# A recurrent layer's boot taken by halves, and a second layer that lags one, two, then three steps

## The chip, the cores and the metric

The kernel runs on one core of a Trainium2 chip. The metric is the device time of one execution, in microseconds (us). It is taken as the median over several executions; a profiled execution beside them gives the trace. In the trace a core has the engines TensorE (PE, with its weight loads as PEld), VectorE (DVE), ScalarE (ACT), GpSimd (POOL) and SyncE (SP), which issues most transfers.

## What is computed

The input is `r, k, v, w` of shape (4, 8, 768, 48) and `u` of shape (8, 48): four sequences, eight heads, 768 tokens, 48 numbers a head. Each head has a state of 48 x 48 that decays by `w` per token. Its result goes through two matrix products with a slight non-linearity between.

```python
for t in range(S):
    cur = einsum('bhd,bhe->bhde', u[None] * kt, vt)
    y[:, :, t] = einsum('bhd,bhde->bhe', rt, state + cur)
    state = wt[:, :, :, None] * state + einsum('bhd,bhe->bhde', kt, vt)
x = y.transpose(0, 2, 1, 3).reshape(3072, 384)
h = x @ w_in            # w_in: 384 x 2048
out = (h - tanh(h)) @ w_out   # w_out: 2048 x 384
```

## The kernel before

The 3072 tokens are cut into eight blocks of 384 (`NB`), two per sequence. Within a block the recurrence works on chunks of 64 tokens (`L`), six per block, and on four pairs of heads (`NPAIR`), a pair filling the partitions. Pairs come in two halves of two (`HALVES` is first pairs 2 and 3, called h1, then 0 and 1, called h2).

For a block the recurrence has these pieces. `behind` (L395) scans w backwards for the decay to the end of each chunk, `take_whole` (L421) picks each chunk's whole decay, `before` (L388) scans forwards from its reciprocal. `times_behind` and `times_before` (L413, L407) multiply them into k and r, and `times_u` (L425) multiplies k by u on ScalarE, in place, after `times_behind` has read it. `gram` (L448) forms the scores of a chunk with itself on TensorE: `own` for a token with itself, `earlier` for earlier tokens; a masked copy on VectorE (L470) puts them into the tile `scores`. `turn` (L481) transposes the decayed keys on TensorE and copies them out on ScalarE into `ks`. `update_1` (L521) multiplies keys and values into each chunk's contribution to the state, for all pairs; `update_2` (L541) walks over the chunks on VectorE, an add and a multiply each. `from_states` and `from_scores` (L591, L610) add up a block's result in PSUM, with a drain and a semaphore (`fence`) between the parts; `result_out` (L645) copies it into the tiles `xT`, and `fill_holes` (L657) moves the rest of the heads, from the tile `late`, by six small transfers.

A block's dense part is a loop of 16 steps f (`NF`), each for 128 of the 2048 middle columns. `first` (L764) does the first layer: three products (six records in the trace) into the single PSUM buffer `hp`, which ScalarE empties into `h`. `slight` (L776) makes g of h: the square s (VectorE, L796), qa (ScalarE, L799), and two products on VectorE (L773). The second layer, in block 0 `Second.add` (L841), multiplies g by `w_out`. In blocks 1 to 7 a scheme with fewer products takes its place (`Fewer`, L877).

The order on every engine but POOL is that of the program text (`manual_schedule`). In the loop (L1121) each step issues, in this order: what was put ahead of h (qa of the step before), `first`, this step's VectorE work, ScalarE's conversion of weights, the next block's pieces of recurrence that `plan` (L945) puts at this step, transfers, and then the second layers that are due. A second layer of block 0 is due three steps after its first layer (L1166, `LAG` 2 plus one).

The weights come as 64-bit patterns and are converted on the chip: `convert` (L249) has three ScalarE pieces and one combining VectorE operation per f. Five buffers hold raw weights. Three of the sixteen conversions lie in the boot, one in step 0 and the rest in steps 1 to 12, each three steps ahead of its use.

`boot` (L1010) prepares block 0, with nothing dense to hide behind. It loads w, k and r by halves, and v; it works the two halves one after the other until the scores, and takes `update_1`, `update_2` and `from_states` for all four pairs at once. `passed` (L288) puts 97 tiny products ahead of the first turn, and `busy` (L281) puts filler products in some places. Before it, memsets and masks are prepared: VectorE sets `scores`, `states` and `ones`, POOL draws all masks, also those which only the general path reads. That path (L1242) is a branch at the end that recomputes everything if a bound was broken; it isn't taken here.

## Time and profile before

| what | us |
|---|---|
| runs | 556.38, 558.57, 558.08 |
| their median | 558.08 |
| the profiled execution | 556.46 |
| its span, first to last instruction | 554.7 |
| first layer of step 0 starts | 29.47 |
| first second layer starts | 40.60 |
| last second layer's records start | 549.21 |

The mean granted clock of TensorE is 0.997. A line of the timeline gives start and duration in us, the engine, the line of the kernel, the operation, the tile written and the tiles read, shapes, and the number of records; in brackets the engine's idle time before and who ended it. A line of the table by windows gives a stretch, its length, the busy time of PE, PEld, DVE, ACT and POOL with their records, the granted clock, the share of the transfer engines and GB/s. Ends of products are modelled, so the distance of two starts is the better measure of what one costs.

### The profile page before, as it was taken

How to read it: one execution, taken by the hardware profiler on the slowest of the kernel's cores; microseconds unless marked ns; L12 is line 12 of the kernel's file. 1: busy time of each engine (PE TensorE's matmuls, PEld its weight loads, DVE VectorE, ACT ScalarE, POOL GpSimd, SP SyncE). 2: the span in 40 equal slices, each digit the busy share in tenths (PEclk: the TensorE clock that was granted, in tenths of full speed). 3: DMA queues.
4: the chain of work that ended last, by engine and by line, in shares of the span. 5: the costliest groups of instructions: out<-in, count | busy, mean ns of one | idle time of the engine just before them, and what ended most of it. 6: DMA issues, size and time to landing. Idle time of an engine off the chain costs nothing.

```text
span 554.7 us, 14151 instructions
## 1 busy us (share of the span) xinstructions
PE 537.9 (97%) x5726; PEld 404.7 (73%) x5726; DVE 463.3 (84%) x947; ACT 402.2 (73%) x811; POOL 12.0 (2%) x40
## 2 busy tenths in 40 slices
PE   4899999999999999999999999999999999999996
PEld 4646566578787787777778787777877777787774
DVE  8789999989989989878997989969897897557563
ACT  3889896697766886688866886688865986666561
POOL 6100000000000000000000000000000000000000
PEclk9999999999999999999999999999999999999999
DMA  8598473244302432236311531136122320100101
GB/s 304 207 320 301 165 215 107 72 122 115 116 13 85 100 118 74 62 94 134 109 54 44 144 116 62 52 89 157 58 88 67 80 65 4 54 1 0 44 2 46
DMA packets 53030, 56.31 MB, mean 102 GB/s; under 512 B 21472, under 2 KB 50912, under 8 KB 52960
## 3 DMA queue, kind: packets, MB, share of 16 engines
q1 hardware_dynamic: 52576, 55.18, 33.6%
q8 instruction: 46, 0.75, 0.5%
q14 instruction: 24, 0.20, 0.1%
q10 hardware_dynamic: 288, 0.10, 0.1%
q0 software_dynamic: 96, 0.07, 0.1%
HBM read 44.73 MB, written 4.72 MB: 89 GB/s over the span
## 4 chain that ended last, share of the span: by engine, by line
PE 94%; ACT 2%; DVE 2%; issue 1%; DMA 1%; SPq 0%; DVEq 0%; ACTq 0%
PE hp L767 44%; PE acc L891 26%; PE att L891 6%; PE acc L844 6%; PE att L463 2%; PE att L603 2%; PE att L620 2%; PE acc L869 2%; PE att L537 2%; DMA r<-in_rT 1%; ACT up L260 1%; PE att L487 1%; DVE scores L470 0%; PE att L285 0%; DVE pre L392 0%
## 5 line engine op out<-in xcount | busy, mean ns | idle before, releaser
L767 PE MATMUL hp<-xT,w_sb 128*128 128x384 f32 x768 | 270.1, 488 | 1.3 <-ACT h L770 1.1
L767 PEld LDWEIGHTS hp<-xT,w_sb 128*128 128x128 f32 x768 | 137.3, 190 | 75.9 <-ACT h L770 3.3
L770 ACT ACTIVATE h<-hp 128x384 f32<-128x384 f32 x128 | 62.7, 490 | 104.8 <-PE hp L767 104.7
L891 PE MATMUL acc<-forms,g 128*128 128x128 f32 x954 | 133.7, 276 | 0.5
L891 PEld LDWEIGHTS acc<-forms,g 128*128 128x128 f32 x954 | 121.6, 192 | 10.3 <-issue 1.3
L773 DVE SCALAR_TENSOR_TENSOR h<-h,s 128x384 f32<-128x384 f32 x128 | 70.7, 552 | 53.9 <-ACT s L788 53.8
L814 DVE TENSOR_TENSOR g<-g 128x256 f32<-128x256 f32 x265 | 103.3, 419 | 7.8 <-PE acc L891 7.0
L789 ACT ACTIVATE qa<-s,shift 128x384 f32<-128x384 f32 x113 | 69.6, 616 | 3.7
L791 ACT ACTIVATE junk<-s,shift 128x384 bf16<-128x384 f32 x113 | 67.7, 600 | 0.0
L773 DVE SCALAR_TENSOR_TENSOR g<-qa,h 128x384 f32<-128x384 f32 x112 | 61.7, 551 | 1.8 <-ACT qa L799 0.2
L788 ACT ACTIVATE s<-h 128x384 f32<-128x384 f32 x113 | 59.1, 523 | 3.6
L891 PEld LDWEIGHTS acc<-w_sb,g 128*128 128x128 f32 x318 | 46.7, 191 | 9.7 <-ACT sums L859 0.3
L891 PE MATMUL acc<-w_sb,g 128*128 128x128 f32 x318 | 53.1, 276 | 0.1
L891 PE MATMUL att<-w_sb,g 128*128 128x128 f32 x212 | 35.5, 275 | 0.0
L891 PEld LDWEIGHTS att<-w_sb,g 128*128 128x128 f32 x212 | 31.1, 192 | 5.3
L926 DVE TENSOR_TENSOR sums<-sums 128x256 f32<-128x256 f32 x84 | 32.9, 408 | 1.6 <-ACT sums L903 1.3
L844 PE MATMUL acc<-w_sb,sums 128*128 128x384 f32 x96 | 33.9, 489 | 0.1
L260 ACT ACTIVATE up<-raw 128x768 f16<-128x768 f32 (+1 forms) x32 | 32.0, 1070 | 0.0
L392 DVE TENSOR_TENSOR_SCAN pre<-w,start 128x780 f32<-128x780 f32 x16 | 28.5, 1783 | 0.5
L403 DVE TENSOR_TENSOR_SCAN post<-w,seed 128x780 f32<-128x780 f32 x16 | 28.5, 1783 | 0.2 <-DMA w<-in_wT 0.2
L844 PEld LDWEIGHTS acc<-w_sb,sums 128*128 128x128 f32 x96 | 17.9, 190 | 12.0 <-issue 0.2
L791 ACT ACTIVATION_READ_ACCUMULATOR junk<-s,shift 128x1 f32 x113 | 21.1, 187 | 0.0
(93 smaller groups left out, 506.5 us busy)
## 6 DMA issues: line engine op xcount, KB each, us to landing
raw<-in_weights SPq DMA_DIRECT2D x16, 768.0 KB, 5.8
w<-in_wT SPq DMA_DIRECT2D x7, 780.0 KB, 4.6
k<-in_kT SPq DMA_DIRECT2D x7, 768.0 KB, 4.5
r<-in_rT SPq DMA_DIRECT2D x7, 768.0 KB, 4.5
v_sb<-in_v SPq DMA_DIRECT2D x8, 576.0 KB, 3.9
k<-in_tokens SPq DMA_DIRECT2D x7, 576.0 KB, 3.9
r<-in_tokens SPq DMA_DIRECT2D x7, 576.0 KB, 4.9
out_y<-sums SPq DMA_DIRECT2D x18, 128.0 KB, 1.8
```

The source lines that it names most:

```text
L260: return lambda: nc.scalar.activation(out=to, in_=of, func=AF.Copy, scale=scale, bias=bias)
L392: return nc.vector.tensor_tensor_scan(out=self.tile("pre")[:, cols], data0=self.tile("w")[:, cols], data1=start[:, 0:n * NCH * LP], initia ...
L767: nc.tensor.matmul(hp, lhsT=w_in_sb[:, f, kc, :], rhs=xT[kc], start=(kc == KC - 1), stop=(kc == 0))
L770: return h, nc.scalar.activation(out=h, in_=hp, func=AF.Copy, scale=1.0 / UPSCALE)
L773: return lambda: nc.vector.scalar_tensor_tensor(out=out, in0=in0, scalar=scalar, in1=in1, op0=op0, op1=ALU.mult)
L788: nc.scalar.activation(out=s, in_=h, func=AF.Square)
L789: nc.scalar.activation(out=qa, in_=s, func=AF.Square, bias=shift[:, 4:5])
L791: nc.scalar.activation(out=junk[:, 0:NB], in_=s, func=AF.Relu, bias=shift[:, 5:6], accum_out=excess[:, at:at + 1])
L814: return lambda: nc.vector.tensor_tensor(out=G[:, to:to + 2], in0=two(G, g_at(q, a0), g_at(q, a1)), in1=two(G, g_at(q, b0), g_at(q, b1)), ...
L844: nc.tensor.matmul(acc, lhsT=g[:, j * P:(j + 1) * P], rhs=w_out_sb[:, f, :], start=(f == self.first), stop=(f == NF - 1))
L891: nc.tensor.matmul(to, lhsT=G[:, g_at(q, a), :], rhs=rhs, start=start, stop=stop, skip_group_check=True)
L926: ops.append(lambda op=op, at=at: nc.vector.tensor_tensor(out=at[0], in0=at[1], in1=at[2], op=OPS[op]))
```

## The change

- The boot loads w of h1 in two transfers, starts with one weight load instead of three, and begins three more behind ScalarE operations. `behind` runs for one pair at a time in h1.
- Each half has its own update (`update_half`), with a drain and a wait between its two passes over a pair of heads. The states of a half come from one scan per pair over 48 x 6 elements (`states_half`), for which ScalarE spreads the decays by column (`totals_by_column`). `from_states` reads these states, six elements apart. A half's result is finished before the other's.
- `own` goes ahead of `turn` in h1, whose copy (`turn_2`) comes later. `passed` is gone. All hole transfers go on SP.
- ScalarE sets `scores` and two small tiles by copies of zeros; the padding columns of `states` are set only in the general path, which also draws masks 1, 2, 4 and 8.
- Conversions in the loop begin one step earlier in number (f + 3 from f = 0), with two of the three ScalarE pieces in one step and the third at the start of the next, for f below 8. One conversion is carried from the boot into step 0.
- In steps 0 to 3 of block 0 square, qa and both products are issued in the step itself, behind the combining operation, and the second layer is due one step later; for steps 4 to 7 two, then three.

```diff
+SOON = 4
...
-    nc.gpsimd.memset(mask_all[0:L], 1.0)
...
+    draw(("diagonal", "above"), slice(0, 128))
...
-    nc.vector.memset(A, 0.0)
+    nc.scalar.copy(out=A.rearrange("s h p c t -> s (h p c t)").rearrange("s (n t) -> s n t", t=BANK),
+                   in_=start[:, 0:BANK].unsqueeze(1).to_broadcast([P, 2 * NPAIR * NCP * L // BANK, BANK]))
...
-        nc.vector.memset(st[:, :, :, D:], 0.0)
...
+        def update_half(self, ps, p0):
+            self.by_column = scratch(ps)[:, :, 0:D * NCH].rearrange("d p (e c) -> d p e c", c=NCH)
+            for x in range(UP):
+                if x:
+                    nc.tensor.drain().then_inc(fence, 1)
+                    fences.append(None)
+                    nc.tensor.wait_ge(fence, len(fences))
+                for c in range(0, NCH, 2):
+                    for h in range(2):
+                        for par in range(2):
+                            p = (x + par) % UP
+                            toks = slice(64 * par, 64 * par + 64)
+                            e0 = (p0 + p) * D2 + h * D
+                            nc.tensor.matmul(self.by_column[64 * h:64 * h + 64, p, :, (c + par + 1) % NCH],
+                                             lhsT=self.ks[toks, p0 + p, c // 2, 64 * h:64 * h + 64],
+                                             rhs=self.v[toks, c // 2, e0:e0 + D], start=True, stop=True)
+        def totals_by_column(self, p0):
+            of = self.whole(p0, UP).rearrange("d (p c) -> d p c", c=NCH)[:, :, 1:]
+            nc.scalar.copy(out=first_totals[:, p0:p0 + UP, :, 1:],
+                           in_=of.unsqueeze(2).to_broadcast([P, UP, D, NCH - 1]))
+        def states_half(self, p0):
+            for p in range(UP):
+                to, by, kv = (t.rearrange("d e c -> d (e c)") for t in
+                              (first_states[:, p0 + p], first_totals[:, p0 + p], self.by_column[:, p]))
+                nc.vector.tensor_tensor_scan(out=to, data0=kv, data1=by, initial=0.0, op0=ALU.add, op1=ALU.mult)
+            return lambda kv=self.by_column: nc.vector.tensor_tensor(
+                out=states[1][:, p0:p0 + UP, 0, 0:D], in0=first_states[:, p0:p0 + UP, :, NCH - 1],
+                in1=kv[:, :, :, 0], op=ALU.add)
...
+        blk.behind(h1 + 1, 1)
+        blk.behind(h1, 1)
         blk.take_whole(h1, UP)
+        blk.totals_by_column(h1)
         blk.before(h1, UP)
         blk.times_behind(h1, UP)
         blk.times_u(h1, UP)
-        blk.turn(ps, h1, ahead=97)
         own = blk.own(ps, h1)
+        blk.turn_1(ps, h1)
         blk.times_before(h1, UP)
         earlier = blk.earlier(ps, h1)
         blk.bound(h1)
         blk.bound(h2)
+        blk.turn_2(h1)
+        blk.update_half(ps, h1)
         blk.behind(h2, UP)
         blk.take_whole(h2, UP)
+        blk.totals_by_column(h2)
         own()
         blk.times_behind(h2, UP)
...
+        begin_behind(blk.times_u(h2, UP), more_weights(nc.sync))
         first_a, first_b = convert(*raws.pop(0))
+        run(first_a[:1])
+        blk.turn_1(ps, h2)
+        begin_behind(blk.turn_2(h2), more_weights(nc.sync))
         second_a, second_b = convert(*raws.pop(0))
         third_a, third_b = convert(*raws.pop(0))
...
+        earlier()
+        blk.results(ps, halved=True)
+        blk.result("from_scores", both[0])
+        blk.states_half(h1)()
+        blk.result("from_states", both[0], True)
+        run(first_a[1:2])
+        blk.before(h2, UP)
+        own = blk.own(ps, h2)
+        blk.update_half(ps, h2)
+        blk.times_before(h2, UP)
+        earlier = blk.earlier(ps, h2, ahead=3)
+        blk.result_out((3,), nc.scalar.copy)
+        blk.fill_holes([nc.sync])
+        later.load("w")
+        run(first_a[2:])
+        blk.result_out((2,), nc.scalar.copy)
         own()
...
+        onwards = blk.states_half(h2)
+        blk.results(ps, halved=True)
+        busy(blk.yp[0][:, 0], 4)
+        blk.result("from_states", both[1])
         earlier()
...
+        onwards()
+        run(second_a[:1])
+        begin_behind(second_a[1](), more_weights(nc.sync))
+        run(second_a[2:])
         run(first_b)
         blk.result("from_scores", both[1], True)
...
+        busy(scratch(ps)[:, 0], 2)
+        begin_behind(third_a[0](), more_weights(nc.sync))
+        later.load("k")
         blk.result_out((1,), nc.scalar.copy)
         blk.result_out((0,), nc.vector.tensor_copy)
...
+        return third_a[2:], third_b
...
-            if i == 0 and f in (1, 2, 3):
+            if i == 0 and f == 1:
                 busy(acc[0], 2)
...
+            if not i:
+                run(carried[0])
+                extra = carried[1]
+            if not i and f < SOON:
+                run(square + ahead_of_h)
+                ops, later_ops, ahead_of_h = extra + later_ops + behind, [], []
+            elif not i:
                 ops = rest + square + formed + extra + behind
...
             if f + READY in converted:
-                ops, extra = convert(*raws.pop(0))
-                for op in ops:
-                    op()
-            elif f:
-                extra = []
+                ops, carried = convert(*raws.pop(0)), []
+                some_now = 2 if f < 2 * SOON else 3
+                run(ops[0][:some_now])
+                carried = ops[0][some_now:], ops[1]
...
-                due.append((now + LAG + (not i), second.add if later else second.added, (f, g)))
+                due.append((now + (LAG if i else 1 if f < SOON else 2 if f < 2 * SOON else 3),
+                            second.add if later else second.added, (f, g)))
```

152 lines of the change are left out of this document (65 added, 87 removed).

## The prediction

> **What bounds the kernel now.** I read the page first (engines and slices), then the table by windows for the start, then the timeline of the first 60 us, and the chain of waits last.
>
> ```profile
> PE 537.9 (97%) x5726; PEld 404.7 (73%) x5726; DVE 463.3 (84%) x947; ACT 402.2 (73%) x811; POOL 12.0 (2%) x40
> ...
> PE   4899999999999999999999999999999999999996
> ```
>
> TensorE is busy for 97% of the span, and only the first slice (13.9 us each) and the last show anything else. The table by windows (stretch, length, then PE, PEld, DVE, ACT, POOL busy, granted clock, DMA share, GB/s) shows where:
>
> ```profile
> 0.00:5.00 5.00, 2.58 (x97) 2.47 (x97) 3.54 (x14) 1.49 (x2) 4.30 (x18) 1.00 0.55 178
> 5.00:10.00 5.00, 0.64 (x3) 0.64 (x4) 4.82 (x6) 0.66 (x2) 4.80 (x6) 1.00 1.03 341
> ...
> 35.00:40.00 5.00, 4.07 (x13) 2.16 (x14) 4.40 (x8) 5.00 (x8) 0.00 (x0) 1.00 0.98 358
> 40.00:50.00 10.00, 10.00 (x41) 6.37 (x40) 9.65 (x19) 9.99 (x16) 0.00 (x0) 1.00 0.92 319
> 50.00:60.00 10.00, 10.00 (x108) 6.19 (x107) 9.56 (x17) 9.28 (x15) 0.00 (x0) 1.00 0.65 209
> ```
>
> From 40 us on TensorE never stops, so the change can win or lose only in what lies before: the boot, and block 0's first steps. But in block 0 VectorE (9.6 of 10) and ScalarE (9.3 to 10 of 10) are nearly full as well. The timeline (start, duration, engine, line) gives the marks:
>
> ```profile
> 4.31 1.78 DVE L403 TENSOR_TENSOR_SCAN post<-w,seed 128x780 f32<-128x780 f32 x1 [0.17 <-DMA w<-in_wT]
> ...
> 9.36 1.54 PE L487 MATMUL att<-ident,post 128*128 128x128 f32 x6 [4.71 <-DVE post L417]
> ...
> 10.84 1.56 PE L463 MATMUL att<-r,k 48*64 48x64 f32 x48
> ...
> 29.47 2.17 PE L767 MATMUL hp<-xT,w_sb 128*128 128x384 f32 x6
> ...
> 40.60 2.10 PE L844 MATMUL acc<-w_sb,sums 128*128 128x384 f32 x6
> ...
> 51.78 1.50 ACT L489 COPY ks<-att 128x768 f32<-128x768 f32 x2
> ...
> 53.62 1.17 PEld L537 LDWEIGHTS att<-v_sb,ks 64*48 64x48 f32 x80 [0.55 <-ACT ks L489]
> ```
>
> The boot ends at 29.47, when the first layer of step 0 starts. A first layer (L767) or second layer (L844) is worth 1.935 us of TensorE (starts 42.54, 44.47, 46.41). By 40.60 TensorE has done four first layers, 7.74 us of work in 11.13: **3.39 us wasted**. So: change = (boot's end moves) + (new waste in block 0 - 3.39).
>
> **The boot.** Times are from the span's start; new ones are estimates laid end to end from rows.
>
> *Prologue.* VectorE loses the memsets of the scores (1.34), the states (0.79, 0.27) and the ones (0.06); it was free at 4.14 and waited for w until 4.31. ScalarE gets three copies: 768 elements take 0.80 and 384 take 0.47, so 1536 cost some 1.5 and the 192s 0.35 each. They end near 4.9, while ScalarE idles until 9.34: free, and if `start` came late, cover until 5.7. Its five-fold broadcast of totals (480 elements, 0.6 per half) sits in idle ScalarE time too. POOL draws 128 of 288 mask columns; its other 4.06 us (3.15 of selects, 0.91 of copy) ended at 10.36, two us before the first mask use: free.
>
> *First half.* w comes in two transfers. 390 KB took 3.4 us from issue; half of it, an estimate between 1.9 (a 24 KB transfer) and 3.4, lands at 2.8 to 4.3, I take 3.6. Two scans of 390 (half of 1.78 plus some 0.07, 0.95) end at 5.5 instead of 6.09. Totals, reciprocal, scan, product take 3.2 as now: times_behind ends at 8.6 (now 9.30), the second half's reverse scan at 11.3 (now 12.00). That is 0.7.
>
> *TensorE's order.* Now "own" comes ahead of "turn". Own starts 0.05 to 0.37 after times_u (8.7 to 10.1), so 10.1; own 1.56, turn 1.5, earlier 1.5: 14.6 (now 13.67). VectorE's masked copies then stand at 11.8 and 14.7, the latter after a wait of 1.1 us. The second half's turn no longer precedes its VectorE work.
>
> *States.* Now: 96 update records 2.21 us, then ten steps of 0.39, 19.08 to 23.0, on all four pairs. New: per half 48 records (0.77 at the pace of 80 in 1.29, 1.1 at that of L537 in the boot) plus a drain between pair halves, unseen in the trace: 0 to 0.8 (a 0.84 LDWEIGHTS wait is the longest near one), I take 0.25. Then two scans of 288 elements, 288/780 of 1.78 plus 0.08 = 0.74 each, and one small add 0.3. So VectorE: earlier copy ends 15.7; scans and add 17.5; reciprocal and scan 19.5; times_before 20.5; own copy 21.4; scans 22.8; earlier copy 23.7. TensorE's from_scores with drain (0.9 + 0.25) ends 24.95, ScalarE's copy-out 25.97, the two remaining thirds of the first layer (0.75 each) 27.6.
>
> *SP.* All six hole transfers now go on SP: 0.62 each instead of three beside POOL's three. `late` is ready at 19.4 (first half's result 18.4, two copies 0.97); issued to 23.2, landed (2.2) by 25.4, needed at 26.7. Of the six weight loads two now start behind ScalarE's times_u and turn copy (15.8, 17.3); with the 6.6 that such a load took up to 45 us they land at 22.5 and 24.0, where ScalarE wants the first at 21.4. That puts the last copy-out 0 to 1 later; I take 0, as loads under less traffic took 4.1. The later w load is issued behind them at 23.2, now 27.53, and its slowest landing (6.1) is 29.3; first use near 31.
>
> Step 0's first layer thus ends at 27.6 against 31.64: **-4.1**. The ends: scans, drains and loads at the high bounds and the slow pace of L537 throughout cost 1.5 of that; w at 2.8 and no wait at 14.7 gain 1.0.
>
> The 97 tiny matmuls end at 4.65, and TensorE then idles 4.7 us. The own group at 10.84 takes 1.56 for 48 records; at 70.65 96 take 1.63. So they leave no faster clock: free to drop. The Trainium skill ("TensorE: Matmul & The Clock Gate", Part 1) says that the array starts at half clock and is released by about 3.4 us of sustained work, and falls back after an idle window. By that, TensorE's work from 10.1 on, denser than now, is released before the states, and the sum stands; at the slow pace throughout, the boot's gain would be the 2.6 of the poor end. The trace agrees with the second half of the rule: after thin work the granted clock falls to 0.50 from 25.5 to 28.9.
>
> **Block 0.** TensorE's work is unchanged, bar four dropped fillers; its order isn't. Second layers of steps 0 to 3 come one step behind, 4 to 7 two, the rest three. So steps 0, 5 and 10 have no second layer; before these were 0, 1, 2. Each such step has a round trip (first layer, ScalarE's h, next first layer, as one hp buffer serves all) of 2.79 for 1.935. In 5 and 10 the turn (1.31) and the earlier group (1.56) fill it. That would save waste; the chain of g charges for it.
>
> One conversion's three ScalarE pieces cost 0.80, 0.92, 0.92, h 0.37, qa 0.50: 3.5 us per step of 3.87. VectorE in steps 0 and 1: square 0.48, combine 0.87, h 0.66, g 0.47, reverse scan with totals 1.89: 4.4. Counting from hp0's start, each engine in its own order:
>
> - g0 ends 5.83 (h0 2.25 to 2.74, third piece, qa 3.54, combine until 4.6, h, g); acc0 could start at 4.73: waste 2.0 (0.85 of it hp1's round trip).
> - acc1 and acc2 wait 0.5 each for VectorE's 4.4 us steps: 3.0.
> - Step 5: ScalarE comes to qa at 21.8, to h at 22.7 (hp5's end), then has three pieces (until 25.7) and only then the turn's two copies (0.75 each, until 27.2). TensorE got there at 25.6, with hp6 done, since no second layer of 1.94 stands between turn and hp6. In the trace before the same wait was 0.1. Price 1.7: 4.7.
> - acc7, two steps behind, meets g7 behind the eleven state steps (4.3 us): 0.6. The masked "earlier" group 0.2.
>
> **Waste 5.5 instead of 3.39: +2.1.** The same walk over the old order gives 3.3, close to 3.39. Bounds: 3.0 if the turn's copies come in time, 7 if each wait is doubled. After step 10 the lag is three as before, with 5 us of slack in the old trace. The general branch isn't taken; POOL's branch at 546.9 lies well ahead of the end, so its new body is free (0 to 0.5).
>
> **Sum.** -4.1 + 2.1 = **-2.0**. The profiled execution took 556.46 (span 554.7, 1.76 around it): 554.5. It is 1.6 below the median of 558.08, on which the sum gives 556.1. I give 555.4, between the two.
>
> **Rivals.**
> - *The copies come in time* (for: ScalarE's rows overlap, and 0.1 of waiting was enough before; against: 9.99 of 10 busy). Block 0 then wastes 3 to 3.4, and the boot's 4.1 stay: 552.4 to 554. Chance 0.30.
> - *The chain of g doesn't shorten: slower.* In the old trace h to g took 4.6, 6.2, 6.0 and 5.7 us in steps 0 to 3. If running square, qa, h and g in one step left it at 6, acc0 would start at 8.3 and each later one 5.1 after (half of 1.94 + 2.25 + 6.0) against 3.87: acc3 at 23.6 with 15.5 of work done, waste 8.1, with the turn's wait up to 9.8. That is +4.7 to +6.4; with -4.1 from the boot +0.6 to +2.3, with its poor end (-2.6) up to +3.8: 557 to 562. It decides from a chain of some 5 us. For: VectorE's 4.4 us steps; against: a third of the conversion and no other step stands in it. Chance 0.13.
> - *Half clock into block 0.* The 48 records at 25.55 took 1.88, those at 19.46 0.89. If TensorE's gaps at 22 to 24 bring that on, first layers of two steps cost 1.94 more each, part of it in gaps: +1 to +3, 555 to 558. Chance 0.07.
> - Forecast: 0.50.
>
> **Numbers.** Within 0.5% (2.8 us, about what a measurement of this kernel can tell from no change) lies most of the forecast and of the clock rival, with some of the first and second; below it most of the first rival and the forecast's good quarter. Faster 0.35, same 0.53, slower 0.12. Range: 551.5 (first rival at the boot's good end) to 559 (the slow rival's middle).
>
> **What would show it.** Right: first L767 near 25 to 26; TensorE unbroken from some 46; waits of acc on g of 0.5 to 1.2 us in steps 1 to 3; L537 waiting for ks by over 1 us in step 6. Wrong: first L767 after 27 (drain, scans, transfers), no wait at ks (first rival), or acc waits beyond 1.5 us in each of steps 1 to 3 (second).

## The result, and the profile after

The changed kernel takes 558.56 us (median of 22 runs) against 556.52 for the kernel before (22 runs beside them): a ratio of 1.0032, 95% interval [1.0016, 1.0048]. I had forecast 555.4, from a sum that gains 2.0; the change lost about as much. That is less than the 0.5% that I called no change, but it is clear of zero and has the wrong sign. The profiled execution took 558.36 with a span of 556.5, which is 1.8 above the span before (554.7), so its trace can stand for the difference.

The page after, the engines' busy time and the 40 slices (13.9 us each) of TensorE:

```profile
PE 534.3 (96%) x5635; PEld 400.6 (72%) x5635; DVE 460.8 (83%) x939; ACT 405.6 (73%) x816; POOL 3.4 (1%) x29
...
PE   3789999999999999999999999999999999999996
```

TensorE has 3.6 us less work than before (the tiny products and fillers that went), and the span is longer: TensorE is idle for 22.2 us instead of 16.8. Of these 5.4 us more, 3.9 lie in the first three slices (2.3 of them in the first, where the tiny products were) and 1.0 between 41.7 and 60 us. The timeline of TensorE in the boot (start, duration, engine, line, operation, records, idle time before):

```profile
20.06 0.33 PE L465 MATMUL att<-pre,post 48*64 48x64 f32 x3
22.56 0.92 PE L465 MATMUL att<-pre,post 48*64 48x64 f32 x45 [2.17 <-issue]
23.41 1.80 PE L291 MATMUL att<-ident 128*128 128x512 bf16 x4
25.14 1.53 PE L645 MATMUL att<-pre,first_states 48*48 48x64 f32 x48
26.94 0.89 PE L663 MATMUL att<-scores,v_sb 64*48 64x64 f32 x48 [0.27 <-PEq L685]
...
29.25 2.17 PE L810 MATMUL hp<-xT,w_sb 128*128 128x384 f32 x6 [0.88 <-ACT xT L697]
```

L465 is `gram`, the second half's earlier group; L810 is the first layer. Three of 48 products run, then nothing for 2.17 us, and the releaser is "issue": the engine waited for nothing that the profile shows. The four fillers behind it take 1.80 (in a boot without the gap, below, 1.04). The first layer of step 0 starts at 29.25, against 29.47 before: the boot gained 0.22, not 4.1. The table by windows has the clock:

```profile
20.00:22.00 2.00, 0.38 (x4) 0.20 (x4) 1.71 (x3) 1.96 (x4) 0.00 (x0) 1.00 0.55 195
22.00:24.00 2.00, 1.44 (x47) 1.04 (x47) 0.48 (x1) 1.64 (x3) 0.13 (x2) 0.88 0.27 76
24.00:26.00 2.00, 2.00 (x35) 1.01 (x37) 1.61 (x3) 0.82 (x1) 0.00 (x0) 0.50 0.78 191
26.00:28.00 2.00, 1.74 (x78) 1.34 (x70) 0.09 (x1) 0.45 (x1) 0.00 (x0) 0.76 1.05 372
```

TensorE is busy for 0.38 of the 2 us from 20 on, and from 24 to 26 it gets half its clock. The raw records of the granted clock are finer: in every trace here, until the work ends, each stretch at half clock lasts 3.41 us or twice that, and each full one behind the first record is a multiple of it. Cut into these steps, the changed kernel's trace reads:

```profile
20.12:23.53 3.41, 1.24 (x50) 1.02 (x50) 1.59 (x4) 3.37 (x5) 0.00 (x0) 1.00 0.39 137
23.53:26.94 3.41, 3.15 (x53) 1.64 (x51) 2.08 (x3) 0.93 (x2) 0.13 (x2) 0.50 0.83 237
```

TensorE is idle for 2.17 us of one step and has half its clock in the next. The trace before has the same gap in the same group, smaller:

```profile
21.53 0.69 PE L463 MATMUL att<-pre,post 48*64 48x64 f32 x30
23.50 0.50 PE L463 MATMUL att<-pre,post 48*64 48x64 f32 x18 [1.28 <-issue]
```

In block 0 the waits of the second layer (L887) and of the update (L545) in the changed kernel:

```profile
35.13 2.20 PE L887 MATMUL acc<-w_sb,sums 128*128 128x384 f32 x6 [0.88 <-DVE sums L816]
39.97 2.20 PE L887 MATMUL acc<-w_sb,sums 128*128 128x384 f32 x6 [0.70 <-DVE sums L816]
44.34 2.20 PE L887 MATMUL acc<-w_sb,sums 128*128 128x384 f32 x6 [0.23 <-DVE sums L816]
56.26 1.62 PE L545 MATMUL att<-v_sb,ks 64*48 64x48 f32 x80 [0.67 <-ACT ks L493]
70.01 2.20 PE L887 MATMUL acc<-w_sb,sums 128*128 128x384 f32 x6 [0.31 <-DVE sums L816]
```

Counted from the start of step 0, TensorE comes to the same place in block 1 (the fifth first layer there) 84.49 us later, before 82.56: block 0 costs 1.93 more, forecast 2.1. Boot -0.22 and block 0 +1.93 give +1.7, close to the +1.8 of the spans.

### The profile page after: what moved, and what is told of

It is laid out like the page before. It is cut to its first block, busy times and chain, and to the rows that moved or that the text cites. A ratio compares the mean times of both kernels' runs of the same rounds, so it can differ in the third digit from the quotient of the medians.

```text
span 556.5 us, 13959 instructions
## 1 busy us (share of the span) xinstructions
PE 534.3 (96%) x5635; PEld 400.6 (72%) x5635; DVE 460.8 (83%) x939; ACT 405.6 (73%) x816; POOL 3.4 (1%) x29
## 4 chain that ended last, share of the span: by engine, by line
PE 86%; DVE 7%; ACT 2%; issue 2%; PEld 2%; DMA 1%; PEldq 0%; DVEq 0%; SPq 0%; ACTq 0%
PE hp L810 41%; PE acc L934 26%; PE att L934 6%; PE acc L887 3%; PE att L663 2%; PE att L465 2%; PE acc L912 2%; PE att L645 2%; PE att L545 1%; DVE w_sb L266 1%; DVE post L403 1%; DMA r<-in_tokens 1%; DVE states L557 1%; ACT up L262 1%; DVE sums L816 1%
## 5 line engine op out<-in xcount | busy, mean ns | idle before, releaser
L810 PE MATMUL hp<-xT,w_sb 128*128 128x384 f32 x768 | 269.9, 488 | 1.1 <-ACT xT L697 0.9
L810 PEld LDWEIGHTS hp<-xT,w_sb 128*128 128x128 f32 x768 | 137.4, 190 | 74.5 <-ACT xT L697 1.3
L887 PE MATMUL acc<-w_sb,sums 128*128 128x384 f32 x96 | 34.2, 492 | 2.2 <-DVE sums L816 2.1
L262 ACT ACTIVATE up<-raw 128x768 f16<-128x768 f32 (+1 forms) x32 | 33.3, 1071 | 0.0
L403 DVE TENSOR_TENSOR_SCAN post<-w,seed 128x780 f32<-128x780 f32 (+1 forms) x17 | 28.5, 1680 | 2.0 <-DMA w<-in_wT 2.0
L887 PEld LDWEIGHTS acc<-w_sb,sums 128*128 128x128 f32 x96 | 17.7, 190 | 16.1 <-DVE sums L816 4.9
```

The lines of the kernel that those rows point to most:

```text
L262: return lambda: nc.scalar.activation(out=to, in_=of, func=AF.Copy, scale=scale, bias=bias)
L403: return nc.vector.tensor_tensor_scan(out=back(t[:, 0:width]), data0=back(self.tile("w")[:, a:a + width]), data1=back(seed[:, 0:width]), i ...
L810: nc.tensor.matmul(hp, lhsT=w_in_sb[:, f, kc, :], rhs=xT[kc], start=(kc == KC - 1), stop=(kc == 0))
L887: nc.tensor.matmul(acc, lhsT=g[:, j * P:(j + 1) * P], rhs=w_out_sb[:, f, :], start=(f == self.first), stop=(f == NF - 1))
```

## The experiments

The theory after the result: TensorE's instructions arrive in pieces of fixed size, and in the boot a piece is used up before the next is there; the transfer that brings it stands behind the weights. The rival: TensorE waits for a buffer or a semaphore that the profile doesn't name. The lines of an edited kernel can lie up to 6 lower than those above. "Rest" in the tables is the span less the start of step 0's first layer: 525.2 before, 527.3 in the changed kernel.

### Does the gap belong to a product, or to a count of instructions?

Two kernels put tiny products ahead of the changed kernel's first own group (n is 97 or 12), one takes the 97 away from the kernel before.

```diff
-        own = blk.own(ps, h1)
+        own = blk.own(ps, h1, tiny=n)
...
-        blk.turn(ps, h1, ahead=97)
+        blk.turn(ps, h1, ahead=0)
```

97 of them. Expected: 

> The changed kernel with the 97 tiny products put back, ahead of the first own group, where TensorE idles until 9.3 us anyway: 194 more TensorE instructions ahead of everything else, no other edit. Theory (instruction supply): the 2.2 us gap in the second half's earlier group comes because TensorE's instruction stream reaches the end of what has been fetched (a 16 KB packet of the instruction queue moves at 20.3, the gap lasts until 22.56). Then its place is fixed by the number of instructions, and it moves 97 products earlier, out of the earlier group into the own group before; the earlier group runs in one piece near 20.1, the clock doesn't fall, step 0's first layer starts at 25.5 to 27, and the time falls by 2 to 4 us. Rival (a wait that the trace doesn't show, on a PSUM buffer or a semaphore of that group): the gap stays at the same records, 2.2 us, first layer at 29.2, time unchanged within 0.3 us.

12 of them. Expected: 

> The same with 12 tiny products, 24 instructions. Instruction supply: the gap moves some 12 records earlier, past the three fillers into the last records of the second half's update, and starts near 18.9 instead of 20.4; update and fillers end after it, at about 21.2, so the state scans start there and the gain is 0 to 1.5 us. Hidden wait: the gap stays behind the third record of the earlier group, at 20.4, and nothing changes.

The kernel before without its 97. Expected: 

> The kernel before without its 97 tiny products. Instruction supply: its gap of 1.28 us, now behind the 30th record of the second half's earlier group, moves 97 products later, to behind the first layer or into the last from_scores group; the earlier group is then in one piece, and some other group near 25 to 29 has a gap of 1 to 2.3 us; time within 1 us of before. Hidden wait: the gap stays behind the 30th record and the time doesn't change. If the tiny products were a warm-up of the clock, the groups at 10 to 17 get slower: own above the 1.56 us that it takes with them.

Measured, TensorE's timeline with 97 (own of the second half, then its earlier group):

```profile
18.77 0.85 PE L471 MATMUL att<-r,k 48*64 48x64 f32 x41 [0.47 <-issue]
...
24.30 0.46 PE L471 MATMUL att<-pre,post 48*64 48x64 f32 x14 [2.16 <-issue]
```

and with 12:

```profile
23.77 0.46 PE L592 MATMUL att<-v_sb,ks 64*64 64x48 f32 x6 [4.21 <-issue]
```

12 products ahead move the gap by 12: from behind the third product of the earlier group, across its three fillers, to six products short of the update's end. 97 move it to behind the sixth product of the own group, and the next gap follows after 42 + 48 + 3 + 34 = 127 products (one more, of 0.36, stands 125 recorded products ahead of the first). In the kernel before, taking 97 away moves its gap from the 30th product of the earlier group to four before the end of the last scores group (1.36 long). So a gap belongs to a count; the rival falls. 127 products with their weight loads are 254 instructions, so that with a few waits and drains a piece is some 256.

The times: 97 tiny products 1.0041 [1.0016, 1.0066], 12 of them 1.0069 [1.0037, 1.0101], the kernel before without any 1.0025 [1.0002, 1.0049]. With 97 and with 12 I had expected a gain, of 2 to 4 and of 0 to 1.5 us; both lost. Twelve products cost more than 97: their gap is 4.21 long. What the transfers have to do with that is the next question. The own group at 10.85 took 1.56 in the kernel before with and without the 97: for it they are no warm-up.

### What holds the piece up

The transfers' queues, in narrow windows, show single packets of 16 KB on a queue for instructions. The first product behind a gap starts 2.2 to 2.6 us after such a packet begins. Two pairs not listed take 2.7 and 3.0 ("late, old" and "queue, old" below); there the packet itself took 1.7 and 2.1 us, in the listed ones 0.9 to 1.4.

| kernel | packet at | gap ends at |
|---|---|---|
| before | 21.2 | 23.50 |
| changed | 20.4 | 22.56 |
| 97 tiny products | 16.5 / 22.0 | 18.77 / 24.30 |
| 12 tiny products | 21.6 | 23.77 |
| three loads early | 16.1 / 20.0 | 18.67 / 22.44 |
| loads late | 20.3 | 22.77 |
| queue of ScalarE, new block 0 | 23.5 | 25.86 |

The Trainium skill ("Runtime: NRT & Kernel Launch", Instruction fetch mechanics) says that an engine refills its instructions in blocks of 16 KiB, 256 instructions, over a transfer queue of its own while it works on the block before, and that crossing a block is mostly hidden. Size, count and queue agree with the packets here. That it is hidden does not: between two gaps the boots by halves use a block in 3.4 to 4.0 us, and TensorE stands still for 0.3 to 4.2.

In the changed kernel the weights of steps 1 and 2 are under way from 15.5 on, most of them until 21.5. So I left those two loads out (steps 1 and 2 then compute with step 0's weights), or began all three ahead of the boot's work, or moved them.

```diff
 # left out
+        if more_weights.n in (1, 2):
+            raws.append((more_weights.n, more_weights.raw, None))
 # early: three ahead
+        for _ in range(3):
             more_weights(nc.sync)
 # in both
-        begin_behind(blk.times_u(h2, UP), more_weights(nc.sync))
+        blk.times_u(h2, UP)
-        begin_behind(blk.turn_2(h2), more_weights(nc.sync))
+        blk.turn_2(h2)
```

Left out. Expected: 

> The changed kernel without the weight loads of steps 1 and 2: both conversions read step 0's raw weights, so these two steps compute with wrong weights; all else is as it was. It takes 1.5 MB away from the transfers between 15 and 23 us. Theory A (the fetch of the next 256 TensorE instructions waits behind bulk transfers): the packet of the instruction queue moves at 18.3 to 19 instead of 20.3, TensorE's gap in the earlier group shrinks from 2.17 to 0 to 0.8, the clock doesn't fall, step 0's first layer starts at 25.5 to 27, and the time falls by 2.3 to 4 us. Theory B (the fetch is only asked for when the stream has run dry, and takes 2.3 us whatever else moves): the gap stays at 2.1 to 2.5, the time within 0.5 us.

Early. Expected: 

> The changed kernel with its weight loads 1 and 2 issued right behind load 0 and not behind ScalarE's times_u and turn copy, as the kernel before does it. The transfers then end near 16.5 and leave 17 to 21 empty. Theory A: the instruction packet for the block that runs dry at 20.4 goes at 18.3 to 19, the gap shrinks to 0 to 0.8, first layer at 25.5 to 27, time down by 2 to 4 us, that is 0.996 to 1.000 of the kernel before; a fetch asked for near 13.5 is later now, but has until 17. Theory B: gap unchanged. A third way: the earlier loads delay v and r of the second half and the boot loses what the gap gives.

Left out, TensorE's timeline:

```profile
20.05 1.24 PE L465 MATMUL att<-pre,post 48*64 48x64 f32 x48
21.23 1.04 PE L291 MATMUL att<-ident 128*128 128x512 bf16 x4
22.19 1.26 PE L645 MATMUL att<-pre,first_states 48*48 48x64 f32 x48
23.72 1.26 PE L663 MATMUL att<-scores,v_sb 64*48 64x64 f32 x48 [0.27 <-PEq L685]
24.92 0.60 PE L291 MATMUL att<-ident 128*128 128x512 bf16 x2
26.36 2.17 PE L810 MATMUL hp<-xT,w_sb 128*128 128x384 f32 x6 [0.83 <-PE att L291]
```

There is no gap, the granted clock stays at 1.00, and the packet that came at 20.4 now came at 17.7. Step 0 starts at 26.36, 2.89 earlier: 2.17 of gap, and 0.7 that fits the stretch at half clock. In both traces the first record of the clock stands at 13.3, so they compare at the same pace. The loads make the gap.

Two limits belong here. The medians show less than the traces: 556.39 without the loads, 2.2 below the changed kernel (measured at another time), and level with the kernel before (1.0002), whose boot in the trace is 3.1 longer and whose rest is 2.2 shorter. And TensorE has done its fillers by 25.5, yet step 0 starts at 26.36: ahead of its first weight load stands a wait of 1.65 us (PEldq is the sequencer that issues weight loads):

```profile
L810 PEldq EVENT_SEMAPHORE  x5: 51/51/1650, 24.5 to 27.2; - x5
```

It runs from 24.54 to 26.19, and VectorE's last copy of xT ends at 26.15. Early loads are no way out: they delay the packet before (16.1 instead of 13.6) and leave gaps of 1.05 and 0.30.

Then the loads moved, with the whole work kept: behind the own copies and the second half's scan ("late"), the same idea in the kernel before, and into the stretches between packets ("between").

```diff
 # late
+        begin_behind(own(), more_weights(nc.sync))                      # step 1
+        begin_behind(blk.before(h2, UP), more_weights(nc.sync))         # step 2
 # the kernel before, late
-        begin_behind(first_a[2](), more_weights(nc.sync))
+        begin_behind(third_a[0](), more_weights(nc.sync))
 # between
+        begin_behind(blk.turn_2(h1), more_weights(nc.sync))             # step 1
+        begin_behind(first_a[1](), more_weights(nc.sync))               # step 2
```

Late. Expected: 

> The changed kernel with its whole work kept; only the start of two weight loads is moved: that of step 1 behind the masked copy of the first own products (ends at 12.3 us in the changed kernel's trace), that of step 2 behind the second half's scan of the starts (ends at 18.5 us). So no weights are in flight in 16.7 to 20.3 us, when TensorE asks for the instructions behind the third product of the second earlier group. Theory (the instructions of TensorE come in pieces and the piece waits behind the weights): the 2.17 us gap in the second earlier group shrinks under 0.4 us, though a gap of up to 0.7 us may come one piece later (24 to 25 us), the clock stays at 1.00, step 0's first layer starts at 26.2 to 27.0 us instead of 29.25, as it did without the loads (26.36), and the span is 553.6 to 554.4 us instead of 556.5. Rival (what the run without loads took away was the wait of the conversions for their weights, not the instructions' wait): conversions here wait for the same loads or later ones, so the first layer starts at 28.5 us or later and the span stays at 556 to 557.

The kernel before, late. Expected: 

> The kernel before the change; only the start of the loads of steps 3 and 4 is moved, from behind the last of the first conversion (20.2 us) to behind the first of the third (22.9 us), that is past the fetch that ends the gap of 1.28 us in its second earlier group. Theory: the gap there falls to 0.3 to 0.8 us (the fetch has its own 2.3 us and no weights before it), the full-clock share of the boot grows, and the first layer of step 0 starts 0.5 to 1.5 us earlier (28.0 to 29.0 instead of 29.47) or, if the last pieces of the conversions bind then, at 29.0 with its six products at the full clock (2.17 instead of 3.49); span 553.2 to 554.4 (554.7). Rival: nothing moves, 554.7 within 0.3, gap 1.2 to 1.3.

Between. Expected: 

> The changed kernel with its whole work kept; the loads of steps 1 and 2 are put into the stretches between TensorE's fetches (packets at about 13.5, 17.5 and 21 us in the run without these loads): that of step 1 behind the first half's copy of the turned keys (ends 13.2 us, so the transfer runs in some 14.4 to 16.6), that of step 2 behind the second conversion piece of step 0 (ends 17.3 us, transfer 18.5 to 20.6). The run before this one that moved them hit the packet at 13.5 us instead (it came at 15.5) and gave 28.6 us for the first layer of step 0. Theory (a piece of 256 instructions waits behind the weights): no gap over 0.5 us in the boot's products, first layer at 26.3 to 27.2 us if TensorE's clock rises by 13 to 14 us as in most runs, span 553.6 to 554.5. Rival (any load in this stretch costs the same, wherever it is put): a gap of over 1 us somewhere between 13 and 26 us, first layer at 28.5 or later, span 556 to 557.

Between, TensorE's timeline:

```profile
16.92 1.53 PE L663 MATMUL att<-scores,v_sb 64*48 64x64 f32 x48
18.73 1.21 PE L645 MATMUL att<-pre,first_states 48*48 48x64 f32 x40 [0.28 <-PEq L685]
...
22.35 0.93 PE L465 MATMUL att<-pre,post 48*64 48x64 f32 x48
...
28.12 1.21 PE L810 MATMUL hp<-xT,w_sb 128*128 128x384 f32 x3 [0.84 <-ACT xT L697]
```

| kernel | ratio | step 0 at | rest | gaps |
|---|---|---|---|---|
| loads left out | 1.0002 [0.9982, 1.0022] | 26.36 | 527.4 | none |
| loads early | 1.0022 [0.9996, 1.0048] | 28.25 | 527.2 | 1.05, 0.30 |
| loads late | 1.0028 [1.0002, 1.0053] | 28.59 | 527.1 | 0.27 |
| the kernel before, late | 1.0052 [1.0030, 1.0074] | 31.18 | 527.5 | 1.48, 0.35 |
| loads between | 1.0005 [0.9988, 1.0022] | 28.12 | 527.2 | none |

The gap under study shrank in each, and two misses show the price of a moved load. In the kernel before, the small transfers into the holes of xT now ran beside the load, and step 0 waited 3.93 for them. With "late" and "between" the span was not the 553.6 to 554.5 that I had written, but 555.7 and 555.3: the scores group, at 16.92 in "between", takes 1.53 and not 0.89. TensorE keeps this slow pace until its first record of the granted clock, which stands at 18.47 in "late" and 19.66 in "between"; in eleven of the sixteen boots by halves it stands at 12.86 to 14.36. This cost the first states' results 2 us. All twelve single runs of "between" show a granted clock of 0.999 or more, the 22 of the changed kernel 0.990 to 0.999; their spans lie at 553.0 to 556.2, in two groups of six, 553.0 to 554.5 and 555.3 to 556.2, which fits an early and a late rise of that pace. The Trainium skill ("TensorE: Matmul & The Clock Gate", Part 1) has a free-running window of 3.4 us that decides on the clock, so that the same kernel rises at different times. The steps of 3.41 us in the traces agree with it; why the busy steps ahead of 15.06 in "late" and 16.25 in "between" brought no rise, no run here shows.

The pace also weighs on the gaps, which I overlooked. A fast boot uses its instructions sooner. "Late, old" below has the same loads as "late" with the rise at 13.30, and there the gaps are 1.11 and 0.57, not 0.27; the kernel before, late, rises at 12.96 instead of 18.68 and has a gap of 1.48 that the kernel before doesn't have. So of late's small gap a part is luck. "Between" stands better: "queue, new" below has its early loads and the rise at 13.97, and no gap until the load that was moved on top.

To test whether earlier work raises the pace, eleven fillers ahead of the first product in "between", and nine in the kernel before.

```diff
-        own = blk.own(ps, h1)
+        own = blk.own(ps, h1, ahead=11)
...
             passed(tp[:, 0], ahead)
+            busy(tp[:, 0], 9 if ahead else 0)
```

Expected, between: 

> The run with the loads between the fetches, and eleven fillers of 128x512 (0.47 us each at half clock, so some 5 us) ahead of TensorE's first product, in a stretch in which it has nothing to do until 9.3 us. In all boots profiled so far the first 48 products take 1.56 us and the later ones 0.9: TensorE came to its full speed at some 12.5 to 15 us in ten kernels and only at 18.4 to 18.7 in the last runs with moved loads, where the first states' results began at 18.7 instead of 16.6 us. Theory (the late rise of TensorE's speed, no gap and no wait, is what keeps the gapless boot from its 26.4 us): with the fillers the first 48 products take 0.9 to 1.2 us, the first layer of step 0 starts at 25.6 to 26.6, the spans of the single runs lose their upper group (555.3 to 556.2 in the run before) and lie at 552.5 to 553.8, ratio 0.995 to 0.998: faster than both kernels. Rival (the fillers' instructions and the quicker use of them bring a gap back, or the speed doesn't depend on earlier work): first 48 products again 1.56 us, or a gap of 1 us or more between 13 and 26 us; span 554.5 or more.

Expected, the kernel before: 

> The kernel before the change with nine fillers of 128x512 behind its 97 tiny products, so some 4.2 us more work ahead of its first transpose (9.36 us). It asks whether the fillers help the boot without halves as much. If the speed comes from earlier work, its first transposes take 0.9 instead of 1.54 us and its first 48 products 0.9 instead of 1.56, but its boot waits for VectorE (0.78 us at 14.45, states until 23.0), so little of that reaches the first layer: span within 0.5 of 554.7, ratio 0.998 to 1.003. Rival: the early speed matters here too and the first layer starts 1 us or more before 29.47.

"Between" with fillers, TensorE's timeline:

```profile
2.07 4.87 PE L291 MATMUL att<-ident 128*128 128x512 bf16 x11 [2.07 <-POOL ident masks.py:199]
9.40 1.08 PE L465 MATMUL att<-r,k 48*64 48x64 f32 x48 [2.46 <-ACT k L428]
...
20.09 0.32 PE L586 MATMUL att<-v_sb,ks 64*64 64x48 f32 x5 [0.75 <-issue]
...
26.75 2.17 PE L810 MATMUL hp<-xT,w_sb 128*128 128x384 f32 x6 [0.88 <-ACT xT L697]
```

The first 48 products took 1.08 instead of 1.56, so earlier work does raise the speed; but the fillers ended 2.46 us too soon, the next groups were slow again (1.45 to 1.56), and the count moved a gap of 0.75 into the update. Step 0 started at 26.75, near the forecast; the ratio, 1.0015 [0.9991, 1.0039], was no better, and in the profiled run a wait for VectorE's scores (1.11 at 88.04) came up in block 1. In the kernel before, the first transposes took 0.88 instead of 1.54 and the first 48 products 0.93; after 2.22 us of idle time the next groups were slow again (1.50 and 1.56). Step 0 started at 27.82 with gaps of 0.26 and 0.86, ratio 1.0017 [0.9991, 1.0042]: single spans from 553.4 to 559.1. Neither settles a gain.

### Block 0

Three kernels take the change's block 0 apart: the old order but the early conversions ("no soon steps"); the new order within a step but the old lag of three; and the whole old block 0 behind the new boot.

```diff
-SOON = 4
+SOON = 0
...
-                due.append((now + (LAG if i else 1 if f < SOON else 2 if f < 2 * SOON else 3),
+                due.append((now + LAG + (not i),
```

No soon steps. Expected: 

> The changed kernel with SOON at 0: in block 0 the second layer lags three steps throughout, square, qa and products stand as in the kernel before, and a conversion's three pieces stay in one step; boot as changed. Theory of the prediction (block 0's new order costs 2 us): the first layer of step 0 stays at 29.2, the waste up to the first second layer is 3.3 to 3.5, no further wait follows, and the time is 1.7 to 2.1 us below the changed kernel, level with the kernel before (0.998 to 1.001 of it). Rival (the loss lies in the boot's aftermath, late weights or a cold TensorE): block 0 loses the same 1.9 with the old order, and the time stays that of the changed kernel.

Old lag. Expected: 

> The changed kernel with a lag of three steps throughout block 0, but square, qa and both products still issued in the step itself, and conversions spread as changed. If the short lag makes block 0's loss (TensorE waits for g), the waste up to the first second layer falls to 3.4 and the time by 1.9 us. If the order on ScalarE and VectorE makes it (qa before two pieces of conversion and before the next h, so that ScalarE waits for the square), the first layers of steps 2 and 3 wait instead: step 2's starts 6.3 after step 0's, step 3's near 11, the waste is 5 to 6 as in the changed kernel, and the time stays within 0.7 us of it.

Old block 0. Expected: 

> The changed kernel's boot with the whole of block 0 as in the kernel before: third conversion finished in the boot, the fourth begun there, lag three, square and qa deferred, fillers in steps 1 to 3. The prediction's second term (block 0's new order costs 2 us) gives: first layer of step 0 at 29.2 to 29.6, first second layer 11.1 later, no waits behind it, 1.6 to 2.1 us below the changed kernel, 0.998 to 1.001 of the kernel before. Rival: more than 0.7 us of the loss remains, and lies in what the boot left late.

With the old lag, TensorE's first layers of steps 2 and 3:

```profile
35.93 2.20 PE L810 MATMUL hp<-xT,w_sb 128*128 128x384 f32 x6 [1.31 <-ACT h L813]
40.60 3.66 PE L810 MATMUL hp<-xT,w_sb 128*128 128x384 f32 x6 [2.47 <-ACT h L813]
```

and ScalarE's qa in the same kernel:

```profile
37.86 0.61 ACT L842 ACTIVATE qa<-s,shift 128x384 f32<-128x384 f32 x1 [1.02 <-DVE top L839]
42.69 0.62 ACT L842 ACTIVATE qa<-s,shift 128x384 f32<-128x384 f32 x1 [1.19 <-DVE top L839]
```

| kernel | ratio | step 0 at | rest |
|---|---|---|---|
| no soon steps | 1.0050 [1.0031, 1.0068] | 29.75 | 527.8 |
| old lag | 1.0059 [1.0034, 1.0083] | 29.62 | 528.7 |
| old block 0 | 1.0031 [1.0012, 1.0050] | 29.84 | 525.3 |

The old block 0 gives 2.0 back in the profiled run (rest 525.3); its median, 558.17, shows nothing of it against the 558.56 of the changed kernel, which was measured at another time. Its step 0 starts 0.6 later: the gap is 2.46 instead of 2.17 and the half clock lasts into more groups, as in the run with the old lag. The kernel with the old lag, measured beside it, has a median of 559.95; its rest is 3.4 longer (528.7 less 525.3), a stretch at half clock in step 3 included, and the short lag wins 1.4 of that back. So it isn't the short lag that costs. By these rows, what costs is what stands ahead of h on ScalarE: qa and two conversion pieces, and in steps 1 and 2 qa also waits 1.0 to 1.2 for VectorE's square of the same step, which stands behind a reverse scan of 1.78. How much of it is qa's place and how much the conversions' earlier begin wasn't separated: in "no soon steps" qa keeps its old place, a carried piece and three more stand ahead of h, and step 2 waited 2.21 and fell to half clock.

### Do the two halves add?

Four kernels join the old block 0 to a boot with less of the gap; the fifth is the last of them with the new block 0. "w later" puts block 1's decays behind step 3's weights; in "queue of ScalarE" these weights start from ScalarE's queue.

```diff
-        later.load("w")
         run(first_a[2:])
...
         run(second_a[:1])
+        more_weights(nc.scalar)                # only queue of ScalarE
         begin_behind(second_a[1](), more_weights(nc.sync))
+        later.load("w")
```

Late loads, old block 0. Expected: 

> The same moved loads with the changed boot, and block 0 as before the change (lag 4, four conversions ahead of step 0, one step's conversion per step). If the two halves of the change add up, the boot ends as in the run above (first layer of step 0 starts at 26.3 to 27.3 us; one conversion more lies ahead of it) and block 0 costs 1.9 us less than in the changed kernel: span 551.6 to 552.9 us, 1.8 to 3.1 under the profiled execution before the change (554.7), ratio 0.994 to 0.998. Rival (block 0's loss was caused by the boot's late end, or the old block 0 needs the time that the boot wins, since its weights come no earlier): waits for weights or a half clock appear in steps 0 to 3 and the span stays at 554 or more.

Between, w later, old block 0. Expected: 

> The same loads between the fetches, block 0 as before the change, and the load of block 1's decays issued behind that of step 3's weights (in the run before this one the fourth conversion waited 2.64 us for them ahead of step 1). If the halves add up: first layer of step 0 at 26.3 to 27.5, step 1 some 2.8 us behind it, block 0 at 1.9 us less than in the changed kernel, span 551.7 to 552.9, ratio 0.994 to 0.998 and so under both kernels. Rival (block 0's old order needs weights earlier than the short boot brings them): a wait of ScalarE for raw in front of step 1, 2 or 3, a half clock behind it, span 554 to 557.

Loads left out, w later, old block 0. Expected: 

> As the run without the loads of steps 1 and 2 (these two steps compute with step 0's weights, so that their part of the result is left out), with block 0 as before the change and the decays of block 1 behind step 3's weights. It asks only whether a boot without gaps and the old block 0 add: no gap over 0.4 us, first layer of step 0 at 26.3 to 26.9, span 551.5 to 552.4 (553.8 in the run with the new block 0, less 1.9), ratio 0.993 to 0.997. If the old block 0 can't follow so early, ScalarE waits for step 3's weights in front of step 1 and the span is 553.5 or more.

Queue of ScalarE, old block 0. Expected: 

> Loads of steps 1 and 2 between the fetches, block 0 as before the change, and the load of step 3's weights begun from ScalarE's queue right behind the first conversion piece of step 1 (about 21.7 us), past the fetch at 21 us and not behind SyncE's six hole transfers (until 23.5); step 4's follows on SyncE, then block 1's decays. In the two runs before, the fourth conversion waited 0.67 to 1.74 us and the fifth 1.23 us for these weights, and one first layer fell to half clock. Theory (the boot without a gap and the old block 0 add if the weights are there): no wait of ScalarE for raw, step 1 some 2.8 us behind step 0, step 10's first layer 39.0 us behind step 0's; span 551.4 to 552.2 if TensorE's speed rises by 15 us, 553.2 to 554.0 if only at 18.5; ratio 0.995 to 0.999. Rival (the old order needs its weights or ScalarE earlier than any short boot can give): again a wait of over 0.5 us in front of steps 1 to 4, span 554.5 or more, ratio 1.000 or above.

Queue of ScalarE, new block 0. Expected: 

> The same loads in the same places with the changed block 0, so that the two differ in block 0 alone. Theory: step 10's first layer 42.8 us behind step 0's less the one second layer that lies ahead of it there, span 1.9 us above the run beside it when TensorE's speed rises at the same time; 553.2 to 554.2 or 555.2 to 556.2, ratio 0.999 to 1.003. Rival (the difference in block 0 came from late weights, not from the order): both runs within 0.7 us.

| kernel | ratio | step 0 at | rest | what came up |
|---|---|---|---|---|
| late, old | 1.0023 [1.0003, 1.0043] | 28.16 | 529.2 | gaps of 1.11, 0.57; 2.64 for weights; step 1 at half clock |
| between, old | 1.0013 [0.9999, 1.0026] | 28.57 | 528.4 | 0.67, 1.23, 0.39 for weights; step 3 at half clock |
| left out, old | 1.0030 [1.0014, 1.0046] | 26.02 | 529.1 | 1.74 for weights; step 1 at half clock |
| queue, old | 1.0019 [0.9994, 1.0045] | 30.17 | 526.1 | gaps of 0.29, 1.48; step 0 at half clock |
| queue, new | 1.0052 [1.0031, 1.0073] | 27.76 | 528.9 | gap of 1.45; step 0 at half clock |

No profiled span came down to what the theory had it at. The shortest boot of all (26.02) gave everything back, in ScalarE's conversion of step 3's weights, as its rival had it:

```profile
29.37 0.89 ACT L262 ACTIVATE w_sb<-raw 128x768 f32<-128x768 f32 x1 [1.74 <-DMA raw<-in_weights]
```

So the halves do not add as they stand: the old block 0 has a fourth conversion ahead of step 1 and needs step 3's weights there, the new one only later. A load from ScalarE's queue cured this wait, and ran into the next fetch (queue, new; TensorE's timeline):

```profile
23.74 0.67 PE L663 MATMUL att<-scores,v_sb 64*48 64x64 f32 x30 [0.27 <-PEq L685]
25.86 0.53 PE L663 MATMUL att<-scores,v_sb 64*48 64x64 f32 x18 [1.45 <-issue]
```

The gap is back, 45 + 4 + 48 + 30 = 127 products behind the old place, again one piece; its packet came at 23.5, without the loads of steps 1 and 2 at 21.5 to 21.7. The first layer of step 0 behind it takes 3.1 (old) and 3.8 (new) instead of 2.2. Less this, the rests are 525.2 and 527.3: with no wait for weights the two block 0 differ by 2.1, so the difference is that of the order and the conversions, not of late weights. None of the eighteen beats the kernel before. With its whole work kept the best is "between", 1.0005 [0.9988, 1.0022].

## Why the prediction was wrong

- **TensorE's order and the states, in the sum of the boot (-4.1): failed.** Up to 20 us the working held or was pessimistic: the first scan starts at 3.52 (3.6), times_behind ends at 8.6 (8.6), own copy of the second half at 20.4 (21.4). (The rows of its end add up to 27.5 and not 27.6, which changes nothing.) But the sum laid groups end to end at the price of their rows and gave the supply of instructions no term, although the trace before showed "1.28 <-issue" inside one of these very groups. The change moves two weight loads ahead of a fetch. That cost 2.17 of gap and 0.7 behind it, at half clock: 2.9 of the missing 3.9, shown by the run without the loads. The sign "first L767 after 27" came, but for none of the three reasons written beside it.
- **"The two remaining thirds of the first layer" (0.75 each): failed, about 1 us.** The first products can't start ahead: without a gap step 0 starts at 26.36, 0.2 after VectorE's last copy of xT, and takes its full 2.2. The wait shown above stands ahead of the first third, which reads none of VectorE's copies; in the program `hp` lies in a pool of PSUM that is opened where the boot's is closed, so it may be waiting for that space. This wasn't tried.
- **SP, weight loads "late by 0 to 1, I take 0": right for what it priced** (ScalarE waited 0.36 for them), blind to what a load costs another queue.
- **Block 0 (+2.1): right in the trace, 1.93, with some luck.** acc0 starts at 5.88 (5.83 forecast), and the waits stood where the working put them. By the distances of starts, which hold more than the idle time alone, acc1 and acc2 cost 0.97 and 0.50 (0.5 each), ks 1.08 (1.7) and acc7 0.59 (0.6): one too low and one too high, so that the sum came out closer than its terms. That what stands ahead of h costs, and not the short lag, was seen only in the run with the old lag.
- **Rivals.** Half clock came, as the third rival had it, but inside the boot (23.5 to 26.9 us), where it cost some 0.7. The chain of g did shorten, and the copies came late, so the other two didn't happen. The likeliest way to a slower time was one that I hadn't listed.

## What to carry to other kernels

A gap that "issue" ends in the middle of a group of small products is a term of its own: count the instructions from one such gap to the next, find the 16 KB packets, and see what bulk transfer runs ahead of them. Before moving a load, list what else needs the transfer engines then: here nearly every moved load found something, a fetch, a small transfer, or a conversion. And a boot that gets shorter pulls forward each due time behind it, so the gain must be checked again at the first weights that are needed.

## What the runs showed of the hardware

- Small products (126 or 127 pairs of weight load and product between two gaps) use up a 16 KB piece in 2.9 to 4.0 us; from the packet's start to the first product behind the gap it takes 2.2 to 2.6 us, or up to 3.0 where the packet itself is slow, and a packet that weights delay comes up to 2.7 us later (20.4 for 17.7).
- Half clock comes in steps of 3.41 us, and what counts is the idle time within one step. In the first 55 us of the 20 traces the clock fell after each of the 17 full-clock steps in which TensorE stood idle for 1.72 us or more, and after none with 1.48 or less. So the gap of 1.45 in "queue, new", with more idle time in its step (2.14 in all), brought half clock; the gap of 2.16 with 97 tiny products, cut by the border of two steps (1.29 and 0.94 idle), didn't.
- The rise to full speed in the boot came at 18.5 to 19.7 us in four of the sixteen boots by halves that were profiled, at 12.9 to 14.4 in eleven, and at 7.2 with fillers. Ahead of this first record the granted clock reads 1.00 although 48 products take 1.56 us instead of 0.89.
